# Two shared PSUM banks for attention's output and the feed-forward products, a third bank for transposes, and pieces from step 50

## The chip, the cores and the metric

The kernel runs on one core of a Trainium2 chip. The metric is device time in microseconds (us) from one launch; lower is better. Five engines work side by side, each through its own instruction stream in order: PE (TensorE: matmuls, and weight loads shown as PEld), DVE (VectorE), ACT (ScalarE), POOL (GpSimd) and SP, which here only issues DMAs. Matmuls write into PSUM, of which the kernel's pools take eight banks, each a tile of 128 partitions x 512 f32 numbers. ACT and DVE read results out of it; the program gives a bank to the next tile once its last reader is done.

## The reference

Three stages, all in f32, one feeding the next:

```python
# 1. attention: q, k, v of (4 batches, 8 heads, 576 tokens, 64), blocks of 64 tokens,
#    a token sees its own block and those before it
scores = where(mask, q @ k.T / 8, -1e9)
attn = softmax(scores);  x = (attn @ v)          # laid out as 2304 tokens x 512
# 2. feed-forward: w_in 512 x 2048, w_out 2048 x 512
r = maximum(x @ w_in, 0);  x = (s * r * r + b) @ w_out
# 3. top-1 mixture: 8 experts of 512 -> 1024 -> 512, each token goes to the one its gate picks
out[token] = gate * (maximum(x @ w1[e], 0) @ w2[e])
```

## The kernel before

**Attention** (`attention`, L21) works on 16 units. A unit is one pair of heads of one batch, and has nine query blocks, so there are 144 steps and eight more that empty the pipeline. In step t the generator issues the scores of block t into an `s` bank (L131), their maximum (DVE) and exponentials (ACT), the sum's reciprocal (DVE) and the scaling of the row (POOL, L169), and, five steps behind, the transposes of the scaled rows (`tp`, L198) into a `t` bank with their copy to SBUF (`pt`, ACT L211). Seven steps behind, when a group of blocks is complete (i = 3 or 8), `pv` (L213) multiplies with v into an `o` bank, and `x_copy` (ACT L236) brings that to SBUF; after the second group the unit's 576 columns go to DRAM (`xT_d`). The q and k of the next unit are transposed in steps i = 4, 5 and 6 (`tw`, `te`, L95 and L125), also into `t` banks; their readers are ACT (L107, L120) and DVE (L88, L90).

Up to step 44 the order of PE, ACT, DVE and POOL is the order of issue, and the PSUM pools are `BANKS_0`: s 3, t 3, o 1, and one for weight conversion. At `ORDERED = 45` these pools are closed and `BANKS_A = (3, 2, 1)` is opened (L1423): s 3, t 2, o 1. `ffn.banks(c2, "a", NH_A)` adds a bank for hidden products (`ph`) and one for projections (`pxa`). From then on a planner with estimated durations chooses each engine's order from priorities (earlier issue first) and from the banks that it believes free; on the chip that order is fixed.

**Pieces** (`_beside`, L554) are feed-forward work issued among attention's steps, for the first six blocks of 256 tokens. A block has one piece that loads x (DMA, then `xh` ACT L382 and `xl` DVE L383), one per pair p of 256 hidden features (`hidden`, L462: 24 matmuls of 256 columns into `ph`, then ACT L480, DVE L481, ACT L482, DVE L483), and two projections (`project`, L542: 6 matmuls of 512 columns per pair into `pxa`, then the copy `rowa`, ACT L569, and a store). The first block has two pairs, the others four: 5 + 5 x 7 = 40 pieces. Piece n is issued in the first step at or after `PIECE_0 + 2.8 n` (L1425) in which the weights that it reads have been converted in issue order, and the units that it reads are done.

**Weight conversion** (`convert`, L431, called by `weights`) brings the weights of four pairs from 64-bit words to a high and a low part, in 16 chunks. From step 45 on one chunk is issued every fourth step (DVE L400, L402, L405, ACT L455, POOL L412, the low part `wil` or `wol`). By these rules the low part of the 14th chunk (second half of pair 3's w_in) is issued in step 73 and that of the 16th in step 81.

After attention the rest of the feed-forward runs (`after`, L573: three late blocks, then the other four pairs of all blocks), beside the router, and then the experts.

Of the kernel before, what the change touches and what calls it, by code (L numbers as in the profile page):

```python
# [9 lines left out]
F32 = mybir.dt.float32  # L10
# [7 lines left out]
P = 128  # L18
# [306 lines left out]
class Banks:  # L325
# [3 lines left out]
    def __init__(self):  # L329
        self.last = {}  # L330
# [16 lines left out]
class SquaredRelu:  # L347
# [4 lines left out]
    def __init__(self, nc, tc, const, xT_d, w_in, w_out, s, b, part_d):  # L352
        self.nc, self.tc, self.xT_d, self.part_d = nc, tc, xT_d, part_d
        self.D, self.FF = w_in.shape
        self.KC, self.NP = self.D // P, self.FF // 256
        self.NB = xT_d.shape[1] // TB
        self.sc = const.tile([P, 2], F32, name="sc")
        self.s, self.b = s, b
        self.wi_d = w_in.bitcast(I32).rearrange("(c p) f -> p c f", p=P)
        self.wo_d = w_out.bitcast(I32).rearrange("(c p) f -> p c f", p=P)  # L360
        self.wi, self.wo, self.wt = {}, {}, {}

    def pools(self, ctx, ph, nx, nr, ng, order, nc_=3):

        kw = dict(reuse_waits="tile")
        pool = lambda n, b_, **k_: ctx.enter_context(self.tc.tile_pool(name=f"m{ph}_{n}", bufs=b_, **kw, **k_))
        bufs = dict(raw=2, cv=nc_, xr=1, x=nx, r=nr, g=ng)
        p = {n: pool(n, bufs[n]) for n in order.split()}
        self.raw, self.cv, self.xr, self.xp, self.rp, self.gp = (p[n] for n in bufs)
# [92 lines left out]
    def hidden(self, x, p, wide=None, seven=False):  # L462

        nc, KC = self.nc, self.KC
        ph = self.ps_h.tile([P, 2, TB], F32, name="ph", tag="h")
        for e in range(2):
            n = 0
            for c in range(KC):
                for w, a in PASSES:
                    nc.tensor.matmul(ph[:, e], self.wi[p][w][:, c, e * P:(e + 1) * P], x[a][:, c],  # L470
                                     start=(n == 0), stop=(n == 3 * KC - 1))
                    n += 1
        shape = [P, 7, P] if wide else [P, 4, P]
        gh = self.gp.tile(shape, F32R, name="gh", tag="gh")
        gl = self.gp.tile(shape, F32R, name="gl", tag="gl")
        if seven:
            self.sevenths(ph, gh, gl)
            return gh, gl
        r = self.rp.tile([P, 4, P], F32, name="r", tag="r")
        nc.scalar.activation(r, ph.rearrange("p e (t n) -> p (e t) n", n=P), AF.Relu)  # L480
        nc.vector.scalar_tensor_tensor(r, r, self.sc[:, 0:1], r, ALU.mult, ALU.mult)  # L481
        nc.scalar.activation(gh[:, 0:4], r, AF.Identity, bias=self.sc[:, 1:2])  # L482
        self.low_last = nc.vector.scalar_tensor_tensor(gl[:, 0:4], r, self.sc[:, 1:2], gh[:, 0:4].bitcast(F32),  # L483
                                                       ALU.add, ALU.subtract)
        return gh, gl
# [68 lines left out]
    def _beside(self, blocks, rows):  # L554
        nc, D = self.nc, self.D
        for blk in blocks:
            x = self.load_x(blk)
            yield blk
            g = []
            n = NA[blk]  # L560
            for p in range(n):
                g.append(self.hidden(x, p))
                yield blk
            for t in range(2):
                px = self.ps_x.tile([P, D], F32, name="pxa", tag="x")
                for p in range(n):
                    self.project(px, g[p], p, t, p == 0, p == n - 1)
                r = rows.tile([P, D], F32, name="rowa", tag="r")
                nc.scalar.copy(r, px)  # L569
                nc.sync.dma_start(self.part_d[blk * TB + t * P:blk * TB + (t + 1) * P], r)  # L570
                yield blk
# [89 lines left out]
TB = 256  # L661
NA = (2, 4, 4, 4, 4, 4)
MORE = 0
NH_A = 1
BANKS_A = (3, 2, 1)
WB_ENG = lambda nc: nc.vector
ORDERED = 45
PLAN = ("1", "2", "3D", "12CL", "3D", "L", "", "C", "")
# [1 line left out]
CONV |= {4: "D", 6: "D"}  # L670
for n in range(ORDERED, 96, 4):
    CONV[n] = "LC123D"
PIECE_0 = 46
PIECE_D = 2.8
WA_ENG = lambda nc: nc.gpsimd
PASSES = ((0, 0), (0, 1), (1, 0))
# [692 lines left out]
@with_exitstack  # L1369
def kernel(  # L1370
    ctx: ExitStack,
    tc: tile.TileContext,
    q: bass.AP,
    k: bass.AP,
    v: bass.AP,
    moe_w_in: bass.AP,
    moe_w_out: bass.AP,
    moe_s: bass.AP,
    moe_b: bass.AP,
    moe2_modality_id: bass.AP,  # L1380
    moe2_w_gate: bass.AP,
    moe2_modality_bias: bass.AP,
    moe2_w1: bass.AP,
    moe2_w2: bass.AP,
    out: bass.AP,
):
    nc = tc.nc
    NT, D = out.shape
    const = ctx.enter_context(tc.tile_pool(name="const", bufs=1))
    dram = ctx.enter_context(tc.tile_pool(name="dram", bufs=1, space=bass.MemoryType.DRAM))  # L1390
    ident = const.tile([P, P], F32, name="ident")
    make_identity(nc, ident)
    xT_d = dram.tile([D, NT], F32, name="xT_d")
    x2_d = dram.tile([NT, D + 1], F32, name="x2_d")
    rt = Router(nc, const, ident, moe2_modality_id, moe2_w_gate, moe2_modality_bias, x2_d)
    part_d = dram.tile([NT, D], F32, name="part_d")
    ex = Experts(nc, tc, ident, rt, x2_d, moe2_w1, moe2_w2, out)
    ffn = SquaredRelu(nc, tc, const, xT_d, moe_w_in, moe_w_out, moe_s, moe_b, part_d)
    c1 = ctx.enter_context(ExitStack())
    w_a = c1.enter_context(tc.tile_pool(name="m_wa", bufs=1, side="right"))  # L1400
    B, H, S, _ = q.shape
    begun = (B - 1) * S // TB + MORE
    with ExitStack() as c2, ExitStack() as early:
        pieces = ffn.beside(c2, range(begun))
        banks = Banks()
        banks.open(early, tc, 0, *BANKS_0)
        plan = [(blk, chunks) for blk in range(begun)
                for chunks in (0, *range(2, 4 * NA[blk], 4), 4 * NA[blk], 4 * NA[blk])]
        emitted = 0
        conv = ffn.convert(w_a, range(max(NA)), WA_ENG(nc))  # L1410
        converted = [next(conv)]

        def weights(step):
            if step in CONV and converted[0] < 4 * max(NA):
                with ExitStack() as behind:
                    for i in banks.last.values():
                        behind.enter_context(tc.issue_after(i.ins))
                    converted[0] = conv.send((CONV[step], banks.f if step < ORDERED else None))

        for step, done in enumerate(attention(nc, tc, c2, banks, ident, q, k, v, xT_d, weights)):  # L1420
            if step == ORDERED:
                early.close()
                banks.open(c2, tc, 1, *BANKS_A)  # L1423
                ffn.banks(c2, "a", NH_A)
            while (emitted < len(plan) and step >= PIECE_0 + emitted * PIECE_D and converted[0] >= plan[emitted][1]  # L1425
                   and done >= H // 2 * (1 + (plan[emitted][0] * TB + TB - 1) // S)):
                next(pieces)
                emitted += 1
        for _ in pieces:
            pass  # L1430

    def free():
        c1.close()
        ex.open_raw(c1)

    def routed():
        rt.early()
        ex.load_early(0)

    ps_g = ctx.enter_context(tc.tile_pool(name="r_ps_g", bufs=2, space=PSUM, reuse_waits="tile"))  # L1440
    rt.open(ctx, tc, ps_g, NT - begun * TB)
    with ExitStack() as c3:
        last = ffn.after(c3, rt, begun, free, routed)
    ex.open(ctx)
    ex.xs = {i: ex.gather(i, NT - TB) for i in range(EARLY)}
    with tc.issue_after(ex.gathered.ins):
        ex.load_early(1)
    with tc.high_priority():
        for _ in rt.block(*last, ex.turn_early):
            pass  # L1450
        rt.finish(ctx, tc)
    ex.run()
# [32 lines left out]
```

## Time and profile before

| what | value |
|---|---|
| time, median of 3 runs | 904.03 us (902.71 to 904.8) |
| the profiled execution's own time | 902.74 us |
| its span, first to last instruction | 901.0 us |
| TensorE's granted clock, mean | 0.998 |

The span is cut here into stretches that the change touches or leaves alone: attention alone up to 80 us; attention with pieces from 80 to 326.3 us (where attention's last `o` matmul starts just before); the last pieces to 341.4 us; the rest of the feed-forward to about 625 us; router and experts to the end. Busy times of PE are of modelled matmul ends, so that a busy PE can still lose time between two starts.

### The profile page before, as it was taken

The page shows a single profiled execution, that of the slowest core. Times are in us where ns is not written, and L with a number is a line of the kernel's source. Part 1 is how long each engine was busy: PE and PEld are TensorE (multiplying, and loading weights), DVE is VectorE, ACT ScalarE, POOL GpSimd, SP SyncE. Part 2 cuts the span into 40 slices and gives each one's busy share as a digit, 9 for nine tenths or more (in the row PEclk, how much of TensorE's full clock was granted, in tenths as well). Part 3 has the DMA queues.
Part 4 walks back from the last instruction along what each step waited for, and adds up shares of the span by engine and source line. Part 5 has one row for each costly group of instructions (what it writes and reads, how often), then busy time and mean ns, then how long its engine had stood idle before and what let it go on. Part 6 is the DMA issues. An engine that isn't in the chain of part 4 may idle for free. (4 is left out here: it accounts for less than half of the span.)

```text
span 901.0 us, 17062 instructions
## 1 busy us (share of the span) xinstructions
PE 873.2 (97%) x5765; PEld 724.2 (80%) x5765; DVE 637.3 (71%) x1490; ACT 569.5 (63%) x1165; POOL 215.7 (24%) x335
## 2 busy tenths in 40 slices
PE   6999988999999999999999999999999999999996
PEld 5767777888888889999999999998477776776775
DVE  5898785455556346778967777767689987776783
ACT  6998877566667544333566655542288776776773
POOL 5675556233324300000000000001034422222110
PEclk9999999999999999999999999999999999999999
DMA  6757432313321134445112212114346797637501
GB/s 160 198 150 205 135 101 77 101 47 82 79 75 28 61 97 131 140 143 183 48 48 71 70 58 61 48 48 176 129 137 244 242 388 244 219 130 258 191 15 37
DMA packets 109481, 113.84 MB, mean 126 GB/s; under 512 B 62679, under 2 KB 80617, under 8 KB 109387
## 3 DMA queue, kind: packets, MB, share of 16 engines
q1 hardware_dynamic: 105579, 100.74, 36.2%
q0 software_dynamic: 3808, 11.94, 3.8%
q8 instruction: 48, 0.79, 0.4%
q14 instruction: 46, 0.38, 0.1%
HBM read 143.58 MB, written 19.80 MB: 181 GB/s over the span
## 5 line engine op out<-in xcount | busy, mean ns | idle before, releaser
L470 PE MATMUL ph<-xh,wih 128*128 128x256 f32 x576 | 165.3, 287 | 0.4 <-ACT xh L382 0.4
L470 PE MATMUL ph<-xh,wil 128*128 128x256 f32 x576 | 162.3, 282 | 2.5 <-POOL wil L412 2.5
L470 PE MATMUL ph<-xl,wih 128*128 128x256 f32 x576 | 162.1, 281 | 0.3 <-DVE rc L177 0.3
L169 POOL TENSOR_TENSOR p<-p,rc 128x64 f32<-128x64 f32 (+2 forms) x144 | 108.5, 760 | 141.8 <-DVE rc L178 97.5
L470 PEld LDWEIGHTS ph<-xh,wih 128*128 128x128 f32 x576 | 108.9, 189 | 4.8 <-issue 2.9
L470 PEld LDWEIGHTS ph<-xh,wil 128*128 128x128 f32 x576 | 109.1, 189 | 3.3 <-POOL wil L412 2.7
L470 PEld LDWEIGHTS ph<-xl,wih 128*128 128x128 f32 x576 | 109.2, 190 | 2.0 <-DVE rc L177 0.6
L152 DVE TENSOR_REDUCE nm<-sc 128x1 f32<-128x288 f32 (+8 forms) x160 | 69.9, 448 | 42.4 <-PE sc L144 34.8
L160 ACT ACTIVATE p<-sc,nm 128x288 f32<-128x288 f32 (+8 forms) x160 | 81.2, 509 | 18.6 <-DVE rc L177 9.2
L1102 DVE TENSOR_TENSOR w1l<-raw,w1h 128x1024 fp32r<-128x1024 f32 x60 | 71.4, 1222 | 20.0 <-ACT w1h L1101 17.2
L1102 DVE TENSOR_TENSOR w2l<-raw,w2h 128x1024 fp32r<-128x1024 f32 x64 | 75.2, 1219 | 9.6 <-ACT w2h L1101 9.4
L1110 POOL DMA_INDIRECT xr<-x_d,gidx_e x2 | 2.3, 1130 | 307.2 <-PE ph L470 306.9
L480 ACT ACTIVATE r<-ph 128x512 f32<-128x512 f32 x44 | 26.3, 599 | 72.9 <-PE ph L470 72.7
L1101 ACT CAST w2h<-raw 128x1024 fp32r<-128x1024 f32 x64 | 65.8, 1052 | 5.1 <-PE py L1205 4.9
L198 PE MATMUL tp<-ident,p 128*128 128x128 f32 x400 | 64.8, 277 | 4.0 <-POOL p L169 1.7
L1101 ACT CAST w1h<-raw 128x1024 fp32r<-128x1024 f32 x60 | 61.4, 1051 | 8.0 <-PE ph L1188 7.2
L211 ACT COPY pt<-tp 128x512 f32<-128x512 f32 (+3 forms) x128 | 62.6, 506 | 3.6 <-PE tp L198 2.6
L481 DVE SCALAR_TENSOR_TENSOR r<-r,sc 128x512 f32<-128x512 f32 x44 | 35.5, 807 | 32.5 <-ACT r L480 32.0
L198 PEld LDWEIGHTS tp<-ident,p 128*128 128x128 f32 x400 | 46.1, 141 | 13.7 <-issue 4.0
L1205 PE MATMUL py<-w2h,hh 128*128 128x512 f32 x128 | 51.4, 402 | 0.0
L227 PE MATMUL o<-pt,raw_v 128*64 128x320 f32 (+4 forms) x448 | 50.3, 364 | 0.6 <-ACT pt L211 0.4
L1216 POOL DMA_INDIRECT out_dram<-y,sidx x15 | 19.9, 1327 | 129.0 <-ACT y L1170 128.7
(309 smaller groups left out, 2296.1 us busy)
## 6 DMA issues: line engine op xcount, KB each, us to landing
raw<-in_moe_w_dram SPq DMA_DIRECT2D x172, 512.0 KB
xr<-xT_d SPq DMA_DIRECT2D x19, 512.0 KB
wr<-in_moe_w_in_dram SPq DMA_DIRECT2D x16, 512.0 KB
wr<-in_moe_w_out_dram SPq DMA_DIRECT2D x16, 512.0 KB
row<-part_d SPq DMA_DIRECT2D x20, 256.0 KB
x_d<-row SPq DMA_DIRECT2D x18, 256.5 KB
xT_d<-x SPq DMA_DIRECT2D x16, 288.0 KB
raw_q<-in_q_dram SPq DMA_DIRECT2D x32, 128.0 KB
```

Of the source, the lines that this page charges most:

```text
L152: ps.last["max"] = nc.vector.tensor_reduce(nm[:, e:e + 1], scs[e][:, 0:w], AX.X, ALU.max, negate=True)
L160: ps.last["exp"] = nc.scalar.activation(pr[:, k0:k0 + w], scs[e][:, 0:w], AF.Exp, bias=nm[:, 0:1], accum_out=sm[:, e:e + 1])
L169: ps.last["scale"] = nc.gpsimd.tensor_mul(pr[:, 0:n], pr[:, 0:n], rc.to_broadcast([P, n]))
L198: nc.tensor.transpose(t[:, e * P:(e + 1) * P], st[u][i][0][:, c * P:(c + 1) * P], ident)
L211: P_COPY(nc, i0)(o, src)
L227: nc.tensor.matmul(o[r, first * D:n], vt[:, c, hh], p[:, first:, c, r], start=(c == 0), stop=(c == cs[-1]))
L470: nc.tensor.matmul(ph[:, e], self.wi[p][w][:, c, e * P:(e + 1) * P], x[a][:, c], start=(n == 0), stop=(n == 3 * KC - 1))
L480: nc.scalar.activation(r, ph.rearrange("p e (t n) -> p (e t) n", n=P), AF.Relu)
L481: nc.vector.scalar_tensor_tensor(r, r, self.sc[:, 0:1], r, ALU.mult, ALU.mult)
L1101: self.nc.scalar.copy(ws[0][c], r)
L1102: self.nc.vector.tensor_sub(ws[1][c], r, ws[0][c].bitcast(F32))
L1205: nc.tensor.matmul(py, hT[a][:, c], self.w2s[w][c // 2][:, c % 2 * D:c % 2 * D + D], start=(t == 0), stop=(t == 3 * KF - 1))
```

## The change

Three edits. `BANKS_A` becomes (3, 3, 2): transposes get a third bank and `o` gets two. The two banks that were set aside for `ph` and `pxa` are no longer opened in this stage; both are taken from the `o` pool under its tag, so attention's output, hidden products and projections share two banks in turn, whichever is free. The later call of `banks` in `after` is as it was, so there `ph` has its own pool again. `PIECE_0` goes from 46 to 50.

```diff
@@ class SquaredRelu, __init__
         self.wi, self.wo, self.wt = {}, {}, {}
+        self.shared = None
@@ hidden
-        ph = self.ps_h.tile([P, 2, TB], F32, name="ph", tag="h")
+        ph = self.ps_h.tile([P, 2, TB], F32, name="ph", tag="o" if self.ps_h is self.shared else "h")
@@ _beside
-                px = self.ps_x.tile([P, D], F32, name="pxa", tag="x")
+                px = self.shared.tile([P, D], F32, name="pxa", tag="o")
@@
-NH_A = 1
-BANKS_A = (3, 2, 1)
+BANKS_A = (3, 3, 2)
@@
-PIECE_0 = 46
+PIECE_0 = 50
@@ the loop over attention's steps
                 banks.open(c2, tc, 1, *BANKS_A)
-                ffn.banks(c2, "a", NH_A)
+                ffn.shared = ffn.ps_h = banks.o
```

## Rows read from the trace of the kernel before

**Rows 1.** Busy time by stretch (us, counts); columns PE, PEld, DVE, ACT, POOL, clock, DMA.
```profile
80.00:108.00 28.00, 27.42 (x195) 22.55 (x196) 21.11 (x61) 21.79 (x63) 15.60 (x27) 1.00 0.54 149
108.00:150.00 42.00, 36.97 (x283) 30.93 (x282) 34.40 (x93) 31.67 (x95) 23.29 (x35) 1.00 0.34 87
150.00:326.30 176.30, 175.27 (x1234) 148.02 (x1232) 91.03 (x295) 113.12 (x326) 57.05 (x120) 1.00 0.24 67
326.30:341.40 15.10, 14.75 (x76) 12.01 (x75) 5.88 (x12) 4.95 (x8) 0.00 (x0) 1.00 0.58 176
...
342.00:600.00 258.00, 258.00 (x1994) 244.37 (x1992) 197.73 (x445) 133.65 (x196) 0.00 (x0) 1.00 0.29 90
```

**Rows 2.** PE's waits by releaser, 108 to 150 us: total, times, longest.
```profile
PE ph L470 <- POOL wil L412: 2.5, 1, 2.5
PE tp L198 <- DVE ql L88: 1.4, 1, 1.4
...
PE tp L198 <- ACT pt L211: 0.5, 1, 0.5
```

**Rows 3.** PE's waits by releaser, 150 to 326 us: all of them.
```profile
PE pxa L545 <- ACT rowa L569: 0.6, 1, 0.6
```

**Rows 4.** Timeline: the wait for the low weights, PE and POOL.
```profile
141.36 0.39 PE L470 MATMUL ph<-xh,wil 128*128 128x256 f32 x1 [2.49 <-POOL wil L412]
...
140.05 1.26 POOL L412 TENSOR_TENSOR wil<-f,wih 128x512 fp32r<-128x512 f32 x1
```

**Rows 5.** Timeline, PE: transposes of q's and k's last tokens, sixth step of four units.
```profile
87.56 0.27 PE L125 MATMUL te<-ident,raw_t 128*128 128x128 f32 x1
...
149.56 0.33 PE L125 MATMUL te<-ident,raw_t 128*128 128x128 f32 x1
```

**Rows 6.** Timeline: a transpose behind the bank of q's, PE, DVE and POOL.
```profile
127.32 0.41 PE L198 MATMUL tp<-ident,p 128*128 128x128 f32 x2 [1.41 <-DVE ql L88]
...
126.05 1.12 DVE L88 SCALAR_TENSOR_TENSOR ql<-tw,qh 64x384 fp32r<-64x384 f32 x2 [0.69 <-ACT qh L107]
...
125.51 0.72 POOL L169 TENSOR_TENSOR p<-p,rc 128x320 f32<-128x320 f32 x1 [1.47 <-DVE rc L178]
```

**Rows 7.** Timeline, PE and ACT: a projection behind the copy of the one before.
```profile
159.64 0.50 PE L545 MATMUL pxa<-woh,gh 128*128 128x512 f32 x1 [0.57 <-ACT rowa L569]
...
157.00 1.05 ACT L382 CAST xh<-xr 128x1024 fp32r<-128x1024 f32 x1 [2.66 <-DMA xr<-xT_d]
```

**Rows 8.** Weight loads' waits for the readers of banks, 150 to 326 us.
```profile
PEld tp L198 <- ACT pt L211: 1.5, 5, 0.5
...
PEld tw L95 <- ACT pt L211: 0.6, 2, 0.4
PEld te L125 <- ACT pt L211: 0.5, 2, 0.3
...
PEld ph L470 <- ACT r L480: 0.4, 2, 0.3
```

**Rows 9.** Busy time by stretch: one unit of attention alone, and later without new pieces.
```profile
66.00:79.50 13.50, 11.70 (x87) 9.06 (x86) 11.55 (x38) 12.30 (x39) 9.96 (x15) 1.00 0.84 223
142.80:150.00 7.20, 7.20 (x54) 5.35 (x53) 6.09 (x16) 7.04 (x22) 3.64 (x6) 1.00 0.33 75
```

**Rows 10.** Groups by line, 85 to 342 us: busy, mean ns of one | idle before.
```profile
L480 ACT ACTIVATE r<-ph 128x512 f32<-128x512 f32 x22 | 13.2, 598 | 24.1 <-PE ph L470 24.0
...
L569 ACT COPY rowa<-pxa 128x512 f32<-128x512 f32 x12 | 7.0, 585 | 20.7 <-issue 10.2 <-PE pxa L545 10.0 <-ACT qh L107 0.5
```

**Rows 11.** The tile o, 80 to 326 us: its copies and who waits for it.
```profile
L236 ACT COPY x<-o x22: 373/396/447, 83.0 to 315.2; 128x320 f32<-128x320 f32 x11, 128x256 f32<-128x256 f32 x11
```

**Rows 12.** Timeline, PE, after attention: the first matmuls of a late block.
```profile
334.90 0.50 PE L470 MATMUL ph<-xh,wih 128*128 128x256 f32 x2 [0.35 <-ACT xh L382]
```

**Rows 13.** Timeline, PE: first and last of three projection matmuls in a row.
```profile
203.45 0.39 PE L545 MATMUL pxa<-woh,gh 128*128 128x512 f32 x1
...
203.92 0.39 PE L545 MATMUL pxa<-woh,gl 128*128 128x512 f32 x1
```

## The prediction

> **What bounds the kernel now.** I read the busy time by stretch first. PE, the engine of the matmuls, is busy in all 258 us of the feed-forward after attention [rows 1], and it leaves 28.00 - 27.42 = 0.58 us idle from 80 to 108 us, 42.00 - 36.97 = 5.03 us from 108 to 150, and 176.30 - 175.27 = 1.03 us from 150 to 326.3. So the work beside attention is bound by PE, and the change moves no matmul out of it: what it can give is those 6.64 us and what hides between matmuls whose modelled ends overlap. What it gives comes through to the end one for one, since the stretch behind it is full. Next I read who ends PE's waits [rows 2, 3], and then the timeline at each [rows 4, 6, 7]. The reader is to see that the stretch of the waits is short: after 150 us the one wait that is listed has 0.6 us.
>
> **The change, part by part.**
>
> *The first piece four steps later.* Piece 9 is the fourth hidden product of the second block. Its weights are ready in issue order in step 73. Before, 46 + 2.8 x 9 = 71.2, so it went out in step 73 itself, the step in which the low half of its weights was issued. The planner's order put its matmuls too early for POOL: `wil` ran from 140.05 us for 1.26 us, and PE stood 2.49 us [rows 4]. After, 50 + 25.2 = 75.2, which is step 76. A step lasts (149.56 - 87.56) / 27 = 2.30 us there (the same transpose in steps 51 and 78, three units apart) [rows 5], so the product comes 6.9 us later than its weights' step and the wait goes: -2.5 us. Its bounds are 0 (the planner pulls the product forward to the same place, or another product meets a late weight) and -2.5.
>
> The price is four steps in which attention is alone, at the pace of one unit: 4 x 13.5 / 9 = 6.0 us. Alone, PE idles 13.50 - 11.70 = 1.80 us of 13.5, 13.3%, because ACT is busy 12.30 of them [rows 9]; with pieces it idles 0.58 of 28, 2.1% [rows 1]. That is 6.0 x 0.112 = +0.7 us. Pieces 10 and 11 wait for the 16th chunk and go out in step 81 before and after, so the same work stands between 80 and 150 us and only its place in it moves. What is delayed comes out of the gap that was behind it (142.8 to 150 us, attention with no new piece, PE 7.20 of 7.20 [rows 9]), so the bounds are 0 and 6.0 x 0.133 = +0.8. The later pieces run three or four steps late, and after the last step three of forty are left, not two. That tail is PE work in either place. It covers the way from the last unit's store to the first late block, whose first matmul came at 334.90 us [rows 12], 8.6 us after 326.3, with 14.75 us of PE work at hand [rows 1]; with one hidden product more the cover grows: 0. SP's queue gets the same DMAs; the loads of x are issued three steps further behind the stores that they read, which can only shorten ACT's wait of 2.66 us for one [rows 7].
>
> *The third bank for transposes.* At 127.32 us a transpose started 1.41 us late, behind `ql`, the last reader of q's bank, that ran from 126.05 us for 1.12 us. Its own input was scaled by 125.51 + 0.72 = 126.23 us [rows 6]. With another bank it could start 127.32 - 126.23 = 1.1 us sooner: -1.0 us. The wait of 0.5 us on the copy `pt` [rows 2] is of the same kind: -0.45. Small ones stand among the weight loads: 1.5 + 0.6 + 0.5 = 2.6 us after 150 us [rows 8]. PE's matmuls before them still run during most of that, as PE idles 1.03 us in all there; I take -0.5, between 0 and -2.6.
>
> *Two banks in turn for three kinds of tile.* One projection stood 0.57 us behind the copy of the one before, since it had one bank; that copy was late because ACT stood at a load of x [rows 7]. With a free second bank it starts at once: -0.5 (bounds 0 and -0.6). Against this stands a wait that the trace of before can't show. Attention's output had a bank of its own, no matmul waited for its 22 copies of some 0.4 us [rows 11], and now it can find both banks taken: one by a projection that is still summing or whose copy ACT has not reached, one by a hidden product behind its ReLU. PE's order is fixed, so behind a `pv` that waits all else waits: scores, transposes, other products. Before, 22 hidden products and 12 projections had a bank for each kind [rows 10] and PE stood once, 0.57 us, or 0.017 us per tile. For all 56 tiles that is 56 x 0.57 / 34 = +0.9 us, which I take because these are the same readers on the same ACT. Its bounds are 0 and 22 x 0.57 = +12.5 us, every output waiting as that projection did. The planner knows of these banks and puts other work first where it sees them taken; only what ACT does later than planned turns into such a wait.
>
> **The sum.** -2.5 + 0.7 - 1.0 - 0.45 - 0.5 - 0.5 + 0.9 = -3.35, say -3.4 us. From the profiled execution's 902.74 us that gives 899.3 us; that execution lies 1.3 us under the median of the runs, 904.03 us, and from the median it gives 900.6 us. I forecast 900.6.
>
> **The rivals.**
>
> A. *Shared banks stall attention: slower.* A `pv` waits behind a projection's or product's reader in every unit. For it: ACT, which frees all three kinds, is busy 31.67 of 42 us from 108 to 150 us [rows 1], and its queue stands for loads of x. Against: after 150 us ACT is busy 113.12 of 176.3 us, and the two private banks together made PE wait only once. At 0.57 us each it takes (2.5 + 1.0 + 0.45 + 0.5 + 0.5 - 0.7) / 0.57 = 7.5 such waits to eat the gain, a third of the 22; at 15 of them the sum is 8.6 + 0.7 - 4.95 = +4.3 us, so 908.4 us, and at 11 it is +2.05 us, so 906.1 us. I put this case at 906.
>
> B. *The next in line is late: no change.* The stretch up to 150 us has ACT at 31.67 and DVE at 34.40 of 42 us [rows 1], and where attention runs without new pieces ACT has 7.04 of 7.20 [rows 9]. A transpose released by a bank then waits for its row, and a new order of the planner brings new small waits. Only the wait for `wil` goes: -2.5 + 0.7 + 0.9 = -0.9 us, so 903.1 us. Against: the listed waits end on banks and on POOL's low weights, with their inputs ready [rows 4, 6]. That the planner, with other banks, arranges PE's work so that the second shared bank is hardly used belongs here too.
>
> C. *All idle time goes.* All 6.64 us with no new wait: 897.4 us. For it: the wait for `wil` delays by its length ACT's and DVE's work behind it. Against: 6.64 - 2.5 - 1.4 - 0.5 - 0.6 = 1.6 us of it belong to none of the four waits above [rows 2, 3], and no edit is aimed at them.
>
> D. *The stretch has hidden headroom.* PE's weight loads fill 148.02 of 176.3 us, 84%, from 150 to 326.3 us, and 244.37 of 258, 94.7%, later [rows 1]. At the later share the stretch would take 148.02 / 0.947 = 156.3 us, 20 us less: 884 us. Against: three projection matmuls start (203.92 - 203.45) / 2 = 0.235 us apart with nothing between [rows 13], where later a matmul starts every 258 / 1994 = 0.129 us [rows 1]. Each has one weight load, so a run of projections is full at a far lower share of loads, and the share tells of the mix of shapes. The Trainium skill, "Perfetto Trace Analysis", section "Identifying the Most-Contended Engine", says to judge TensorE's headroom by the share of weight loads and not by busy matmuls; this trace does not bear that out for so mixed a stretch.
>
> **How the numbers follow.** Forecast 46%, with its own range of 898.5 to 902.5 us; C 8%; D 1%; B 26%; A 19%. A measurement of this kernel can tell about 0.2%, 1.8 us, from no change, so faster is under 902.2 us and slower over 905.8 us. Faster takes nearly all of the forecast (45%), C and D: 54%. The same takes B and the rest of the forecast: 27%. Slower is A: 19%. The range starts at 896.5 us, a little under C, and ends at 907 us, past the price of A at eleven waits; beyond it lie D, A with more waits than thirteen, and a planner's order that loses elsewhere.
>
> **What would show it.** Right: PE's idle time from 80 to 150 us falls from 5.6 us to 2 or 3; no wait of a hidden product on `wil` of over 1 us; no transpose behind `ql`; attention's last output comes at about 320 to 324 us, as three pieces are left behind it, and PE has 17 us or so of work there; the stretch from then on keeps its length but for that. Wrong: waits of `o` matmuls on `r`, `rowa` or `x` that add up to over 2 us, which is A; the same idle time under other releasers before 150 us, which is B; or a first piece whose matmuls don't come 6 us later than at 78.5 us, in which case the planner pulls it forward and the price of the later start was wrong.

## The result, and the profile after

The changed kernel takes 895.12 us (median of 4 runs, 894.53 to 895.36); the kernel before, run beside it, 904.41 us (4 runs, 902.71 to 905.62). The ratio is 0.9898, 95% interval 0.988 to 0.9915: 9.3 us faster. The forecast was 900.6 us with a range from 896.5: the sign was right, but 3.4 us were forecast where 9.3 were measured. The profiled execution of after took 895.36 us, 7.4 us less than that of before, at the same mean granted clock of 0.998; before's profiled execution lies at the fast end of its runs, after's is the slowest. What lies between 7.4 and 9.3 us may in part be TensorE's clock, which is taken up below, at the start from step 48.

The head of the page of the kernel after:

```profile
span 893.6 us, 17065 instructions
...
PE 869.2 (97%) x5765; PEld 723.3 (81%) x5765; DVE 639.0 (72%) x1490; ACT 567.0 (63%) x1165; POOL 216.6 (24%) x335
```

Busy time by stretch, kernel after; columns as in [rows 1], to which these answer:

```profile
80.00:108.00 28.00, 27.44 (x200) 22.76 (x197) 26.72 (x68) 23.72 (x67) 16.74 (x25) 1.00 0.58 166
108.00:150.00 42.00, 41.10 (x306) 34.84 (x305) 31.77 (x98) 32.36 (x98) 25.65 (x39) 1.00 0.39 103
150.00:312.50 162.50, 161.61 (x1154) 137.64 (x1153) 86.39 (x275) 106.08 (x307) 54.13 (x114) 1.00 0.24 66
312.50:332.40 19.90, 19.90 (x127) 17.37 (x124) 9.49 (x15) 7.96 (x12) 0.00 (x0) 1.00 0.53 161
342.00:600.00 258.00, 258.00 (x1999) 244.53 (x1998) 196.95 (x446) 132.54 (x194) 0.00 (x0) 1.00 0.27 86
```

From 108 to 150 us PE leaves 0.90 us idle instead of 5.03. PE's waits by releaser from 80 to 152 us, kernel after, all of them, beside [rows 2]:

```profile
PE tp L198 <- ACT pt L211: 0.6, 2, 0.4
PE o L227 <- ACT pt L211: 0.4, 1, 0.4
PE pxa L546 <- POOL wol L413: 0.4, 1, 0.4
PE tw L95 <- ACT pt L211: 0.2, 1, 0.2
```

The waits for `wil` and behind `ql` are gone. From 150 to 332 us, beside [rows 3], the projection behind `rowa` is gone too:

```profile
PE pxa L546 <- POOL wol L413: 0.4, 1, 0.4
PE sc L141 <- ACT p L160: 0.2, 1, 0.2
```

Four moments on the timeline, kernel after: the first piece's first matmul, attention's last output, the first matmul of the first late block, which follows the work left behind attention, and a new wait far behind (the wait before the instruction in brackets):

```profile
84.38 0.28 PE L471 MATMUL ph<-xh,wih 128*128 128x256 f32 x1
...
311.57 1.15 PE L227 MATMUL o<-pt,raw_v 128*64 128x320 f32 x12
...
331.80 0.38 PE L471 MATMUL ph<-xh,wih 128*128 128x256 f32 x1
...
700.27 0.43 PE L1239 MATMUL pts<-ident,sx 32*128 32x32 f32 x4 [1.05 <-DVE xl L1125]
```

The first piece's first matmul on the timeline, kernel before:

```profile
78.53 0.28 PE L470 MATMUL ph<-xh,wih 128*128 128x256 f32 x1
```

Now the reading that idle time alone does not give. The first `px` matmul comes when all of attention and the same number of products are done: 1937 matmuls from 66 us on in before, 1936 in after. Busy time by stretch up to that matmul (and, ahead of it, up to 108 us), kernel before:

```profile
66.00:108.00 42.00, 39.32 (x282) 31.68 (x282) 33.16 (x100) 34.59 (x102) 26.06 (x41) 1.00 0.63 171
...
66.00:349.33 283.33, 274.23 (x1937) 230.57 (x1937) 169.49 (x505) 187.49 (x531) 106.40 (x195) 1.00 0.34 92
```

The same, kernel after:

```profile
66.00:108.00 42.00, 39.86 (x290) 32.19 (x289) 38.74 (x110) 36.30 (x109) 27.21 (x44) 1.00 0.63 181
...
66.00:340.38 274.38, 270.44 (x1936) 230.01 (x1934) 170.82 (x506) 185.39 (x531) 107.00 (x195) 1.00 0.34 95
```

The stage is 8.95 us shorter. PE's idle time fell by 5.16 us (283.33 - 274.23 = 9.10; 274.38 - 270.44 = 3.94), and its *busy* time by 3.79 us with the same matmuls, while the weight loads took what they took, 230.57 and 230.01 us. Behind the stage the span gives 1.5 us back (551.7 to 553.2 us). The wait of 1.05 us at 700.27 us, in the stage of the experts, is not in the profile of before, which has 0.7 us of other waits there. What lies behind the stage took 550.7 to 553.7 us over the profiles of all kernels here, none of which edits it, so I read nothing further from that.

### The profile page after: what moved, and what is told of

It is laid out like the page before. It is cut to its first block, busy times and chain, and to the rows that moved or that the text cites. A ratio compares the mean times of both kernels' runs of the same rounds, so it can differ in the third digit from the quotient of the medians.

```text
span 893.6 us, 17065 instructions
## 1 busy us (share of the span) xinstructions
PE 869.2 (97%) x5765; PEld 723.3 (81%) x5765; DVE 639.0 (72%) x1490; ACT 567.0 (63%) x1165; POOL 216.6 (24%) x335
## 5 line engine op out<-in xcount | busy, mean ns | idle before, releaser
L144 PE MATMUL sc<-kh,qh 128*128 128x256 f32 (+5 forms) x128 | 50.8, 397 | 0.6 <-ACT p L160 0.6
```

Source lines behind the costliest of these rows:

```text
L144: scored[0] = nc.tensor.matmul(sc[:, 0:max(w, 256)], a[:, i - 2].rearrange("p h d -> p (h d)"), kk[:, k0:k0 + max(w, 256)], start=(j == 0) ...
```

## The experiments

Theory: the start takes away the wait for `wil` and little else; the third bank of transposes gives more than PE's idle time shows; two banks in turn cost nothing. Rivals: the start gives most of it by another way (less of something beside attention's fullest stretch); it is the number of banks, not which tile has them. The expectations on record name the theories as they stood at the time. All ratios are to the kernel before, run in the same series (its medians there 903.64 to 904.75 us). In the second column a plus stands between banks of their own, and o stands for output, products and projections together. Idle and busy are PE's from 66 us to the first `px`, in the profiled execution; together they are the length of the stage. The last two columns are of the transposes `tp` alone: the idle time before the weight loads of 275 of them, from 80 to 341 us, and the busy time of all 300 from 66 us to the first `px`.

| kernel | s, t, o banks | start | median us | ratio (95%) | idle | busy | loads | `tp` busy |
|---|---|---|---|---|---|---|---|---|
| before | 3, 2, 1+1+1 | 46 | 903.64-904.75 | 1 | 9.10 | 274.2 | 9.0 | 48.6 |
| start alone | 3, 2, 1+1+1 | 50 | 899.31 | 0.9954 (0.994-0.9967) | 5.62 | 274.5 | 8.9 | 49.2 |
| banks alone | 3, 3, 2 | 46 | 899.96 | 0.9962 (0.9948-0.9975) | 9.11 | 271.0 | 4.2 | 46.3 |
| after | 3, 3, 2 | 50 | 895.12 | 0.9898 (0.988-0.9915) | 3.94 | 270.4 | 5.3 | 46.9 |
| one bank unused | 3, 2, 2 | 50 | 897.86 | 0.9935 (0.9922-0.9949) | 5.33 | 273.6 | 9.1 | 49.0 |
| third shared | 3, 2, 3 | 50 | 897.62 | 0.9939 (0.9925-0.9953) | 5.12 | 274.3 | 9.0 | 49.0 |
| `o` private | 3, 3, 1+1 | 50 | 897.64 | 0.994 (0.9926-0.9953) | 6.42 | 271.6 | 5.4 | 47.1 |
| scores two, shared three | 2, 3, 3 | 50 | 906.14 | 1.0041 (1.0026-1.0056) | 10.92 | 274.5 | 8.6 | 46.1 |
| scores two, transposes four | 2, 4, 2 | 50 | 909.21 | 1.0068 (1.0052-1.0083) | 12.04 | 275.6 | 6.4 | 45.8 |
| block 0 early | 3, 3, 2 | 50, block 0 46 | 897.31 | 0.9919 (0.9905-0.9932) | 5.74 | 271.2 | 7.4 | 47.4 |

**1 and 2. Each half alone.** Start alone is the kernel before with one line changed; banks alone is the kernel after with the other.

```
-PIECE_0 = 46        # start alone, in the kernel before
+PIECE_0 = 50
...
-PIECE_0 = 50        # banks alone, in the kernel after
+PIECE_0 = 46
```

> The old banks (transposes two, attention's output, hidden products and projections one each) with the later start alone, PIECE_0 = 50. Theory 'start' (the later start ends the wait for the late low weights and moves work out of the stretch in which ACT and DVE are loaded): if it is the small part that I forecast, -2.5 + 0.7, about 902.6 us against 904.4 before; if it is the main part, 895 to 898 us, with PE's idle time from 80 to 150 us at 2 us. Theory 'banks' (what was gained comes from the banks): 904 to 905 us, PE still waiting for a bank of the transposes.

> The new banks (transposes three, output, hidden products and projections two in turn) with the old start, PIECE_0 = 46. Theory 'banks': 896 to 898 us, with a wait of a hidden product on the low weights of about 2.5 us still in the trace and no transpose waiting on a bank. Theory 'start': 903 to 905 us. If the two parts add, this run and the one with the start alone are together 9.3 us under twice the time before.

They gave 4.3 and 3.7 us, each between the ranges of the two theories: each half carries part of the gain. Together they give a little more than their sum (the start is worth 899.96 - 895.12 = 4.8 us once the banks are there). In the profiled executions the stage is 3.2 us shorter with either half and 8.95 with both. Busy time by stretch, start alone:

```profile
66.00:108.00 42.00, 38.54 (x285) 31.43 (x284) 38.38 (x109) 35.87 (x107) 25.49 (x42) 1.00 0.67 180
108.00:150.00 42.00, 41.14 (x309) 34.60 (x308) 32.25 (x98) 33.70 (x102) 25.45 (x38) 1.00 0.36 98
...
66.00:346.13 280.13, 274.51 (x1936) 230.92 (x1935) 170.61 (x504) 186.89 (x530) 106.03 (x195) 1.00 0.34 93
```

Busy time by stretch, banks alone:

```profile
66.00:346.11 280.11, 271.00 (x1936) 231.55 (x1935) 169.16 (x505) 185.68 (x531) 106.06 (x195) 1.00 0.34 93
```

PE's waits by releaser from 80 us to the `te` of step 78, which comes at 145.28 us there, start alone:

```profile
PE tp L198 <- ACT pt L211: 1.2, 2, 0.7
PE tp L198 <- DVE ql L88: 0.5, 1, 0.5
PE sc L144 <- ACT p L160: 0.4, 1, 0.4
```

and two of the kernel before, up to its `te` at 149.56 us [rows 5]:

```profile
PE sc L141 <- ACT p L160: 0.9, 2, 0.6
...
PE ph L470 <- DVE rc L177: 0.3, 1, 0.3
```

The wait for `wil` is gone, 0.9 of the 1.4 us behind `ql`, and these two of before. The two halves work on different columns of the table. The start takes 3.5 us of idle time and nothing of busy time. The banks take 3.2 us of busy time and, over the stage, nothing of idle time: PE's waits by releaser in banks alone, 80 to 152 us, show that the wait for `wil` stays and that, with the wait behind `ql` gone, a `te` waits 1.6 us:

```profile
PE ph L471 <- POOL wil L413: 2.5, 1, 2.5
PE te L125 <- ACT x L236: 1.6, 1, 1.6
PE sc L141 <- ACT p L160: 1.0, 2, 0.9
```

**3, 4 and 5. Which bank is worth what**, all from step 50. `o` private gives attention's output one bank and products and projections one between them; third shared gives the third bank to the tiles in turn; the last leaves a bank unused.

```
-BANKS_A = (3, 3, 2)
+BANKS_A = (3, 3, 1, 1)      # o private
-                ffn.shared = ffn.ps_h = banks.o
+                ffn.shared = ffn.ps_h = banks.f
...
+BANKS_A = (3, 2, 3)         # third shared
...
+BANKS_A = (3, 2, 2)         # one bank unused
```

> Later start and three banks for transposes, but attention's output keeps a bank of its own and hidden products and projections share the one that is left. Theory 'third transpose bank' (its waits, hidden between matmul starts, are most of the gain): 895 to 897 us. Theory 'sharing' (two banks in turn let the planner run longer stretches of one kind): most of the gain goes, 899 to 903 us, with matmuls waiting on the readers r and rowa.

> Later start, two banks for transposes as before, and output, hidden products and projections share three in turn. Theory 'third transpose bank': 900 to 902 us, with the waits of transposes on the copies pt and on q's last reader back. Theory 'sharing': 894 to 896 us, like the changed kernel or better.

> The changed kernel without the third transpose bank: transposes two, output, hidden products and projections share two in turn, one bank is left unused. Against the changed kernel only that bank differs. Theory 'transpose bank' (the weight loads of transposes wait for a bank while PE still seems busy): 898.5 to 900 us, 3.5 to 5 us over the changed kernel, the transposes' loads back at 9 to 10 us of idle time. Theory 'sharing' (fewer, longer runs do it): 895 to 897 us.

With seven banks, two of them in turn in the place of three private ones, the kernel takes 1.45 us less than start alone in median, though the two intervals meet: giving up a bank cost nothing. All three runs lie outside the ranges of their theories, between them: third bank and sharing each do a part. The bank that seven leave free is worth nothing as a third shared one (897.62 against 897.86) and 897.86 - 895.12 = 2.7 us as a third for transposes (in the profiled executions the stage is 278.95 - 274.38 = 4.57 us shorter with it). Idle time before the transposes' weight loads, 80 to 341 us, by line and form (busy, mean ns | idle before and its releasers), kernel before:

```profile
L198 PEld LDWEIGHTS tp<-ident,p 128*128 128x128 f32 x275 | 32.0, 140 | 9.0 <-issue 3.5 <-POOL raw_v L69 1.7 <-ACT pt L211 1.5
```

the kernel after:

```profile
L198 PEld LDWEIGHTS tp<-ident,p 128*128 128x128 f32 x275 | 32.2, 140 | 5.3 <-issue 1.7 <-POOL p L168 0.8 <-ACT pt L211 0.4
```

and scores two, shared three (experiment 6, three banks for transposes):

```profile
L198 PEld LDWEIGHTS tp<-ident,p 128*128 128x128 f32 x275 | 32.1, 141 | 8.6 <-issue 3.4 <-POOL p L169 3.1
```

Busy time of the tile `tp` alone, from 66 us to the first `px`; columns PE, PEld, ACT, clock, DMA. One bank unused:

```profile
66.00:344.95 278.95, 49.01 (x300) 34.85 (x300) 46.65 (x96) 1.00 0.34 94
```

and the kernel after:

```profile
66.00:340.38 274.38, 46.91 (x300) 34.99 (x300) 46.38 (x96) 1.00 0.34 95
```

As long as the scores have three banks and block 0's pieces move with the others, the load gaps tell the two arrangements apart: 8.9 to 9.1 us with two banks for transposes, 4.2 to 5.4 with three, and the stage is busy for 273.6 to 274.5 us with two and 270.4 to 271.6 with three. But the gaps are not the busy time. With block 0 early they are 7.4 us and the stage is busy for only 271.2; with two score banks they are 8.6 and 274.5, three banks for transposes notwithstanding. What goes with the third bank in every kernel of the table is the transposes' own busy time, 48.6 to 49.2 us with two banks and 45.8 to 47.4 with more: 2.1 us of the 3.2 between one bank unused and after. The rest stands with the other tiles, and a third of the gaps ("issue") has no releaser in the profile, so how the bank does it is argued and not shown.

The `o` private kernel loses 2.5 us against after. PE's waits by releaser, 80 to 340 us, of that kernel:

```profile
PE ph L471 <- ACT r L481: 1.3, 2, 0.7
PE pxa L546 <- ACT rowa L570: 1.0, 1, 1.0
PE pxa L546 <- ACT r L481: 0.5, 1, 0.5
```

One bank for two kinds waits 2.8 us for its readers; with two banks for three kinds no matmul waited for any of these.

**6 and 7. The score banks.** The same number of banks, one of them taken from the scores.

```
-BANKS_A = (3, 3, 2)
+BANKS_A = (2, 3, 3)      # scores two, shared three
...
+BANKS_A = (2, 4, 2)      # scores two, transposes four
```

> The changed kernel with one of the three score banks given to the shared pool: scores two, transposes three, shared three. If the shared pool of two still makes output and products wait (theory 'sharing'): 1 us or more under the changed kernel, 893 to 894 us. If it is enough, scores wait more for exponentials and it is slower: 896 to 899 us.

> The changed kernel with one of the three score banks given to the transposes: scores two, transposes four, shared two. Theory 'transpose banks': the weight loads of transposes, which stood 9.4 to 9.8 us idle with two banks and 5.5 to 6.5 with three, fall to 4 us or less, and the time falls by 1 to 2 us unless scores lose as much: 893 to 897 us. If a third bank is all that they use: the loads stay at 6 us, and the time is that of the two score banks alone, 896 to 899 us.

906.14 us, ratio 1.0041 (1.0026 to 1.0056), and 909.21 us, 1.0068 (1.0052 to 1.0083): both slower than the kernel before, and 7 us or more above what was expected. PE's waits by releaser, 80 to 345 us, scores two and transposes four:

```profile
PE sc L141 <- ACT p L160: 4.3, 3, 1.7
PE tp L198 <- POOL p L169: 2.4, 3, 1.5
PE sc L144 <- ACT p L160: 1.4, 3, 0.9
```

Scores wait for the exponentials that free their banks, and what follows them in PE's order waits with them; PE's idle time in the stage is 12.0 us (10.9 in the other), against 3.9 in after. Rival A's mechanism, a matmul of attention that waits for ACT to free a bank and holds up the queue, exists, at the scores and not at the outputs.

**8, 9 and 10. The start, step by step**, with the new banks.

```
-PIECE_0 = 50
+PIECE_0 = 48      # and 52, and 54
```

> The changed kernel with pieces from step 48. By its times piece 9 goes out in step 74, one step after its weights. Theory 'one wait': most of the gain is there, 895.5 to 897 us. Theory 'the stretch': half of the way between 46 and 50, about 897.5 us.

> The changed kernel with pieces from step 52. Start 54 was 2.3 us over start 50. If that is a price that grows with each step without pieces: about 896.3 us. If it comes at one place only, where the work before step 81 no longer fits: 895 us or 897.4 us.

> The changed kernel with the pieces begun at step 54 instead of 50. Theory 'price of the start' (attention alone costs PE 13% idle): four more steps cost +0.7 us and no wait is left to take away: 895.8 us or a little more. Theory 'moved out of the loaded stretch' (the fewer pieces run beside the weight conversion the better): 893 to 894.5 us.

48: 897.63 us, ratio 0.9927 (0.9912 to 0.9943); 52: 897.14, 0.9927 (0.9912 to 0.9942); 54: 897.44, 0.9935 (0.992 to 0.995). With 46 at 899.96 and 50 at 895.12 the best of those tried is 50. At 48 a wait of 2.5 us for `wil` is still there, and its trace shows what can follow one. Timeline, then busy time by stretch (the clock is the third number from the end), start 48:

```profile
137.95 0.38 PE L471 MATMUL ph<-xh,wil 128*128 128x256 f32 x1 [2.46 <-POOL wil L413]
...
138.00:140.00 2.00, 2.00 (x12) 2.00 (x12) 0.00 (x0) 0.00 (x0) 0.81 (x3) 0.64 0.00 0
140.00:142.00 2.00, 2.00 (x10) 2.00 (x10) 1.08 (x2) 1.32 (x3) 0.00 (x0) 0.51 0.00 0
```

Right behind PE's idle time of 2.46 us the granted clock falls to 0.51, the lower of its two levels (1.2 GHz instead of 2.4), and by 142 us it is back at 1.00. The profiled execution of before has the same wait and no fall [rows 1]. Its other runs have no trace, but a mean clock: 0.996 or less in 18 of the 43 runs of these series, which took 904.4 us on average, and 0.998 or 0.999 in 12, which took 902.8. (In the profiled executions of before and after, with 0.998, the clock falls only at the very end, behind the last matmul, where it costs nothing.) A mean of 0.996 or less was seen only in the three kernels with the wait of 2.5 us (before, banks alone, start 48) and in the two with two score banks, and in none of the 62 runs of the other twelve. By that the wait costs some runs about 1.5 us beyond its length. That the clock falls at this place in those runs too fits, but is not shown. Medians of the three kernels hold it; the profiled executions of before, after and banks alone do not.

Past 50 the stretch of attention alone has a price: PE's waits of the scores, 80 to 340 us, from step 52

```profile
PE sc L141 <- ACT p L160: 1.8, 4, 0.8
```

and from step 54

```profile
PE sc L141 <- ACT p L160: 2.8, 4, 1.1
```

**11 and 12. Piece 9 alone held back**, from step 73 to step 76, all else beginning at 46: with the banks of before and with the new ones.

```
-            while (emitted < len(plan) and step >= PIECE_0 + emitted * PIECE_D and ...
+            while (emitted < len(plan) and step >= PIECE_0 + emitted * PIECE_D + (4.8 if emitted == 9 else 0) and ...
```

> The kernel before with one piece moved: piece 9, the fourth hidden product of the second block, goes out in step 76 instead of 73; start and banks as before. Theory 'one wait' (the later start gains by the wait for the late low weights and little else): 2.5 us under before, about 901.2 us, and the 2.49 us are gone from the trace. Theory 'the whole stretch moves' (the later start gains since all pieces come later against the weight conversion): -1 us or less, with a wait of the same size at another place.

> New banks, old start 46, and piece 9 alone held back to step 76. With the old banks that hold gave 1.1 us, not 2.5. Theory 'next in line' (there the released PE ran into waits on banks and on exponentials): with the new banks it gives the whole 2.5 us, about 897.5 us. Theory 'the stretch as a whole': again some 1 us, about 899 us, and the rest of the later start's 4 to 5 us is in the other pieces.

With the banks of before 902.22 us, ratio 0.9988 (0.9979 to 0.9997): 1.1 us by the ratio, 1.4 by the medians, for a wait of 2.5. With the new ones 897.29 us, 0.9925 (0.9911 to 0.9938), 2.7 us less than banks alone. PE's waits by releaser, 80 to 152 us, piece 9 held with the banks of before:

```profile
PE tp L198 <- DVE ql L88: 1.3, 1, 1.3
PE sc L141 <- ACT p L160: 1.1, 3, 0.6
```

The product no longer waits, and the wait behind `ql` is still there: removing the largest wait did not move the others. With the new banks more came through in the medians, but the medians of the kernels with the wait hold the lower clock too. In the profiled executions the stage is 283.33 - 282.81 = 0.52 us shorter with the banks of before and 280.11 - 278.90 = 1.21 with the new ones. That the transposes' bank lets more of the wait through fits both; that it lets all of it through is not shown.

**13, 14 and 15. What else the start moves.** In the kernel after, one group of pieces at a time is put back to where start 46 had it: the first block's five, piece 9, and all behind piece 11.

```
+ step >= PIECE_0 - (4 if emitted < 5 else 0) + emitted * PIECE_D          # block 0 early
...
+ step >= PIECE_0 - (2.8 if emitted == 9 else 0) + emitted * PIECE_D       # piece 9 early
...
+ step >= PIECE_0 - (4 if emitted > 11 else 0) + emitted * PIECE_D         # late pieces early
```

> The changed kernel with the five pieces of the first block alone put back to the old start (46 + 2.8 n), all others as changed. Theory 'first block' (its work beside the first steps after 45, where ACT is nearly full, costs the 2.3 us that the later start gives beside the wait for the low weights): about 897.4 us. Theory 'second block' (it is the hidden products beside the weight conversion): 895 us, no change.

> The changed kernel with piece 9 alone put back to step 73, the step of its low weights. Theory 'one wait': 2.5 us over the changed kernel, about 897.6 us, with a wait for wil of 2.5 us back in the trace. If the planner now has other work for PE there: 895 to 896 us.

> The changed kernel with all pieces from the third block on (12 to 39) put back to the old times, those before as changed, so that two pieces are left after attention as before. My account has nothing of the gain there: 894.5 to 895.8 us. If the lateness of the late pieces matters (cover of the tail, or products that no longer collide): 896.5 us or more.

Block 0 early: 897.31 us, ratio 0.9919 (0.9905 to 0.9932), 2.2 us over after. Piece 9 early: 897.71, 0.9921 (0.9907 to 0.9934), 2.6 over. Late pieces early: 895.89, 0.9902 (0.9887 to 0.9917), 0.8 over, which by the intervals can't be told from nothing. Together 5.6, against 4.8 for the whole start; pieces 5 to 8 were not put back by themselves. PE's waits by releaser, 80 to 152 us, block 0 early:

```profile
PE tp L198 <- POOL p L169: 2.2, 4, 1.0
```

and piece 9 early:

```profile
PE ph L471 <- POOL wil L413: 1.6, 1, 1.6
```

Of the wait for `wil` only 1.6 us are back there, where 2.5 were expected.

With block 0's pieces in their old place the transposes wait for their scaled rows, four times, behind no bank: the work of the first block no longer stands where attention can use it as filling. That is how the row reads; a kernel that takes away the scaling's lateness was not run.

## Why the size was wrong

**The step that failed first: "The first piece four steps later".** Its sum was -2.5 + 0.7 = -1.8 us; start alone measured -4.3 and, with the new banks, -4.8. The wait for `wil` was sized right as idle time (2.5 us gone), but what its end is worth depends on the rest: taken away alone it gave 1.1 to 1.4 us, and putting piece 9 back into the kernel after costs 2.6. The price was sized right too, but only for the banks of before: up to 108 us PE idles 42.00 - 38.54 = 3.46 us in start alone, 0.78 more than before's 2.68. With the new banks the same four steps cost nothing: 42.00 - 39.86 = 2.14 us, less than the 2.83 of banks alone. What I left out is the rest of the pieces. I wrote that "the same work stands between 80 and 150 us and only its place in it moves" and gave its place no value. It had one: from 108 to 150 us start alone idles 0.86 us, 4.17 less than the 5.03 of [rows 1], where I had taken 2.5. The other 1.7 go with the 0.9 us behind `ql`, which I had counted under the third bank, and with the waits of a score on `p` (0.9) and of a product on `rc` (0.3), which in rival C I had as aimed at by no edit; some of it comes back as waits on `pt` (0.5 to 1.2). With the new banks it is block 0's pieces (2.2 us) that carry most of the rest of the start's gain. And the medians of before hold the runs in which the clock was lower, for which the forecast had no term: in the profiled executions, without it, start alone shortens the stage by 3.2 us.

**The step that failed second: "The third bank for transposes".** Its sum was -1.95 us; one bank unused against after measured -2.7. The two waits it was built on are gone, but the start alone takes most of the `ql` wait already. The bank's real worth is in what I priced at -0.5 "as PE idles 1.03 us in all there". I took PE's idle time for the limit of what small gaps can give. It is not: the same matmuls are busy 274.2 us in before and 270.4 in after, and the transposes among them 48.6 and 46.9. The weight loads' gaps had pointed there, 9.0 us before the transposes' loads alone, more than the three rows of [rows 8] that I added up.

The Trainium skill, "Perfetto Trace Analysis", section "Identifying the Most-Contended Engine", says that busy matmul time of TensorE is no good measure of how close a kernel is to its roofline, since pipelined instructions look smaller in a trace. The share of weight loads I had set aside with rival D, whose 20 us were indeed not there. That busy time is no such measure this trace bears out: 3.79 of the 8.95 us came out of busy time, and the share of weight loads in the stage rose from 230.57 / 283.33 = 81% to 230.01 / 274.38 = 84%, not to the 94.7% of the later stretch.

The Trainium skill, "Perfetto Trace Analysis", section "Optimization Strategy", says that a gap which repeats on the engine that should be saturated can mean too little SBUF or PSUM for the next tile. The trace agrees, with the addition that the repeated gap stood on the weight loads and not on the matmuls: 275 transposes, 9.0 us, 5.3 with a third bank.

**"Two banks in turn for three kinds of tile".** I took -0.5 for the projection and +0.9 for new waits, +0.4. The projection's wait went. The new waits did not come: in after no matmul of a product, a projection or an output waits behind `r`, `rowa` or `x`, and seven banks with two in turn were 1.45 us faster in median than three private ones. The bound of 12.5 us that kept the range wide on the slow side was never near. Rival A needed outputs to wait, and they did not.

**What was right.** PE's idle time from 80 to 150 us was to fall from 5.6 to 2 or 3; it fell to 0.56 + 0.90 = 1.46, further than that. The first piece comes 84.38 - 78.53 = 5.85 us later, as said (6). Attention's last output ends at 312.7 us, not 320 to 324, and up to the late block at 331.80 us some 19 us of PE work remain, all busy, where I said 17 (before: 14.75): the tail costs nothing. That attention ends 13.6 us earlier is 9 us of gain, and the rest more work left behind it. The full stretch behind lets the stage's gain through, to within the 1.5 us above.

**The sum against the measurement.** By runs: start -4.3 (forecast -1.8), two banks in turn -1.45 (forecast +0.4), third bank -2.7 (forecast -1.95): -8.5, the rest of the 9.3 being the scatter of the kernel before between series (903.65 and 904.41 us). By estimate some 0.9 us of the start's -4.3 is the clock in runs of before (903.65 us against the 902.8 of those with 0.998 or more). Rival C, with all idle time gone at 897.4 us, came closest, but by its number alone: idle time was not the bound that I took it for, and not all of it went. In the stage 3.94 us are still idle, and 3.79 us went elsewhere.

## What to carry to other kernels

Don't price a bank on PE's idle time alone: compare the busy time of the same count of matmuls, of the stage and of the tile that gets the bank, since here it differed by 2 to 4 us with no wait listed. A later start moves every piece behind it; value each group's new place, not only the one wait that prompted it. Before adding a bank ask which tile's readers are late: the same bank was worth 2.7 us here with the transposes, nothing with the shared tiles, and taking it from the scores to give it to the transposes cost 8.5 (897.62 to 906.14).

## What was not expected of the hardware

PE's busy time for the same 1936 or 1937 matmuls of this stage, at a granted clock of 1.00, is not a constant: 273.6 to 274.5 us in the kernels of the table with two banks of transposes, 270.4 to 271.6 with three beside three score banks, 274.5 with three beside two. The transposes' own 300 matmuls took 48.6 to 49.2 us with two banks and 45.8 to 47.4 with more.

One wait of 2.46 us of PE, in a stretch that was otherwise full, was followed by a fall of the granted clock from 1.00 to 0.51 in one profiled execution (start 48); a wait of 2.49 us was followed by none in another (before). The runs of before with a mean clock of 0.996 or less took 1.5 us more than those with 0.998 or more.
